# Batch 0's keys and values laid nine tokens to a partition, loaded on one queue, with v cast on the engines and the key sums taken as a column of v

## The chip, the core and the metric

The kernel runs on one core of a Trainium2 chip. The metric is device time in microseconds, the median of the runs. Five engines work side by side, each through its own list of instructions: TensorE (PE, with its weight loads as PEld), VectorE (DVE), ScalarE (ACT), GpSimd (POOL) and SyncE (SP). Sixteen DMA engines move data for all of them; a transfer is issued by an engine and then runs on its own.

## The reference

Inputs are q, k and v of shape (8 batches, 8 heads, 576 tokens, 64), a scale vector g of 512 and two weight matrices (512 x 2048 and 2048 x 512), all float32.

```python
q_s = exp(q) / sum over the 64 columns of a head
k_s = exp(k) / sum over the 576 tokens        # for each head and column
kv  = k_s^T v                                 # 64 x 64 for each batch and head
x   = q_s kv, heads side by side              # 8 x 576 x 512
xn  = (x - mean) / sqrt(var + 1e-6) * g       # over the 512 columns
out = x + relu(xn @ w1) @ w2
```

The maxima that the reference takes off before exp cancel in the quotients, and the kernel leaves them out.

## The kernel before

A batch is worked on as four tiles of 128 tokens (512 tokens, a partition holding four tokens in a row); the last 64 tokens of all eight batches form a ninth group, `C9`. For each batch the kernel builds kv, then x, then x normalised and transposed (`xnT`), and runs the two layers of the MLP. From batch 1 on the products of the layers are combined from seven instead of eight block products (lines 762 and 604); the first batch uses plain products (`mm1_part`, line 520, and `mm2_stream`, line 556). The order on every engine is the order in which the code issues (a manual schedule): `run(main, side)` walks the list of an MLP's matmuls, each with a weight, and issues side work when the sum of weights reaches the work's position.

What comes first is written out by hand in `first_batch`. Only there, batch 0's kv takes all 576 tokens at once: k and v lie six tokens to a partition (`T0 = 6`, so 96 partitions).

- SP issues q of tiles 0 and 1 (line 970) and then k, two heads a time (line 980). POOL waits for q by a small copy into `gate` (line 1004), and then issues v, cast to bfloat16 on the way (line 1006), q's tiles 2 and 3, and the weights: w1's first 512 columns in two halves of rows (line 1013), the rest of w1 and w2 (`load_w1`, `load_w2`), and the loads of batch 1.
- TensorE warms up on zeros (`warm`, line 867). ScalarE takes exp of q and of k. VectorE normalises q of tiles 0 and 1 (`norm_q`), and `eq_pT` transposes them on TensorE (line 928) into `eqT`.
- `z0_mm` (line 306) forms the key sums: exp(k) against a column of ones, six matmuls for each pair of heads; `recip_z` takes the reciprocals. `kv0_mm` (line 321) multiplies exp(k) and v of two heads into a 128x128 product, of which only the two diagonal 64x64 blocks are wanted; one VectorE instruction (line 322) scales it, masks it by `diag` and sums each row. That row sum becomes `mbc` (lines 327 and 331), a 128x128 matrix of -sum/512, by which a matmul takes off the mean of x.
- `xT_mm` (line 342) forms x minus its mean, already transposed, for tiles 0 and 1; `xT_out` (lines 351 and 353) writes it to `xnT` times g: column blocks 0 and 1 on VectorE, 2 and 3 on ScalarE.
- Tiles 2 and 3 of q come later: `eq_pT`, then `q0_rest(t)` (`z_q`, line 940, sums exp of q on TensorE from `eqT`, and `po_mm`, line 414, forms x), `x_fast` (line 464), `x_normed` and `xn_pT`.

The first layer of batch 0 (`mlp_steps(0)`) begins with 16 matmuls on tiles 0 and 1, of which the first eight use w1's first half of rows (kh=0) and the next eight the second half (kh=1); then block 0 for tile 2, then "the second block" (columns 512 to 1023 of w1, tiles 0 and 1), then block 0 for tile 3, and so on. A matmul of this layer has weight 0.5 for two tiles, so position 4 in the side list is after the first eight.

Of the kernel before, what the change touches and what calls it, by code (L numbers as in the profile page):

```python
# [20 lines left out]
def kernel(  # L21
# [50 lines left out]
    ident = const.tile([P, P], BF16)  # L72
    eps_ln = const.tile([P, 1], FP32)
    gate = const.tile([P, 4], FP32)
    ones = const.tile([P, 1], BF16)
    junk = const.tile([P, P], BF16)
    scrap = const.tile([P, 512], BF16)
    bones = const.tile([P, 2], BF16)
    ones_w = const.tile([P, P], BF16)
    diag = const.tile([P, P], FP32)  # L80
    mbc = const.tile([P, NP, P], BF16)
# [204 lines left out]

    kvbox = {}

    def exp_k0(j):
        hs = slice(2 * j, 2 * j + 2)  # L290
        if j == 0:
            eks[0] = raw.tile([P, T0, H, D], BF16, tag="kt", name="ek0", bufs=1)
        nc.scalar.activation(
            eks[0][0:P0, :, hs, :].rearrange("p t h d -> p h t d"), raws[0][0][0:P0, hs], AF.Exp
        )

    def k0_mm(j, t):
        hs = slice(2 * j, 2 * j + 2)
        return eks[0][0:P0, t, hs, :], raws["v0"][0:P0, hs, t, :], P

    def z0_mm(j):

        if j == 0:
            kvbox["z0"] = mm_ps.tile([P, NP], FP32, tag="m", name="z0")
        for t in range(T0):
            nc.tensor.matmul(
                kvbox["z0"][:, j : j + 1], k0_mm(j, t)[0], ones[0:P0],
                start=(j == 0 and t == 0), stop=(t == T0 - 1), skip_group_check=True,
            )

    def recip_z():
        kvbox["rz"] = sml.tile([P, NP], FP32, tag="rzk", name="rzk")
        kvbox["sum"] = sml.tile([P, NP], FP32, tag="lnv", name="kvs")
        nc.vector.reciprocal(kvbox["rz"], kvbox["z0"])

    def kv0_mm(j):
        pool, tag = (att_ps, "a") if j < 2 else (mm_ps, "m")
        pkv = pool.tile([P, P], FP32, tag=tag, name="pkv")
        for t in range(T0):
            lhsT, rhs, w = k0_mm(j, t)  # L320
            nc.tensor.matmul(pkv[:, 0:w], lhsT, rhs, start=(t == 0), stop=(t == T0 - 1))
        nc.vector.scalar_tensor_tensor(
            kv_sb[:, 0, j, :], in0=pkv, scalar=kvbox["rz"][:, j : j + 1], in1=diag,
            op0=ALU.mult, op1=ALU.mult, accum_out=kvbox["sum"][:, j : j + 1],
        )
        if j < NP - 1:
            nc.scalar.activation(
                mbc[:, j], ones_w, AF.Copy, scale=kvbox["sum"][:, j : j + 1]
            )
        else:  # L330
            nc.vector.tensor_scalar_mul(
                out=mbc[:, j], in0=ones_w, scalar1=kvbox["sum"][:, j : j + 1]
            )
# [21 lines left out]
    halves = (slice(0, 64), slice(64, P))  # L355

    def kv_pairs(b, ts=range(T + 1)):

# [501 lines left out]
        for _, fn in side[done:]:  # L860
            fn()

    def warm(n):

        w = mm_ps.tile([P, 4, P], FP32, tag="m", name="warm")
        for _ in range(n):
            nc.tensor.matmul(w, junk, junk[:, 0:4].to_broadcast([P, 4, P]), start=True, stop=True)

    def prep_fast(b):

# [74 lines left out]
    def eq_pT(c, t, eng):  # L945
        pe_T(eqTs[c], eqs[c][0][:, t].rearrange("p h d -> p (h d)"), t, eng)
# [10 lines left out]
    def first_batch():  # L957

        nc.scalar.preload_act_table_set("natural_log_exp_and_others")
        raws[0] = (  # L960
            mlp.tile([P, H, T0, D], FP32, tag="hT", name="kt0", bufs=1), None,
            raw.tile([P, H, T, D], FP32, tag="qt", name="qt"),
        )
        k0, _, q0 = raws[0]
        v0 = mlp.tile([P, H, T0, D], BF16, tag="hs", name="v0", bufs=1)
        raws["v0"] = v0

        def load_q0(t, tn, eng):
            ts = slice(t, t + tn)
            eng.dma_start(  # L970
                q0[:, :, ts],
                q[0, :, 0:SM, :].rearrange("h (p t) d -> p h t d", t=T)[:, :, ts],
            )

        def src0(x, h0, hn):
            return x[0, h0 : h0 + hn].rearrange("h (p t) d -> p h (t d)", t=T0)

        load_q0(0, 2, nc.sync)
        for h0 in range(0, H, 2):
            nc.sync.dma_start(  # L980
                k0[0:P0, h0 : h0 + 2].rearrange("p h t d -> p h (t d)"), src0(k, h0, 2)
            )
        raws["g"] = outp.tile([KO1, P], FP32, tag="ot", name="g_rows")
        nc.scalar.dma_start(
            raws["g"], bass.AP(moe_g_ln.tensor, moe_g_ln.offset, [[P, KO1], [1, P]])
        )
        nc.vector.memset(junk, 0.0)
        nc.vector.memset(eps_ln, 1e-6)
        nc.vector.memset(ones, 1.0)
        nc.vector.memset(bones, 0.0)  # L990
        nc.vector.memset(bones[0:64, 0:1], 1.0)
        nc.vector.memset(bones[64:P, 1:2], 1.0)
        nc.vector.memset(ones_w, -1.0 / DM)
        nc.vector.memset(diag, 0.0)
        for ps in halves:
            nc.vector.memset(diag[ps, ps], 1.0)
        nc.vector.memset(kv_sb[:, 1:B], 0.0)
# [7 lines left out]
        for h0, hn in ((0, 4), (4, 2), (6, 2)):  # L1005
            nc.gpsimd.dma_start(  # L1006
                v0[0:P0, h0 : h0 + hn].rearrange("p h t d -> p h (t d)"), src0(v, h0, hn)
            )
        for t in range(2, T):
            load_q0(t, 1, nc.gpsimd)  # L1010
# [17 lines left out]
        for j in range(NP):  # L1028
            exp_k0(j)
            z0_mm(j)  # L1030
            if j == NP - 2:
                g_columns()
        recip_z()
        kv0_mm(0)
        kv0_mm(1)
        kv0_mm(2)
        xT_mm(0, 0)
        kv0_mm(3)
        exp_qt(0, 2)
        exp_qt(0, 3)  # L1040
        xT_mm(1, 0)
        xT_mm(2, 0)
        xT_mm(0, 1)
        xT_mm(3, 0)
        xT_out(0)
        xT_out(1)
        eq_pT(0, 2, nc.scalar)
        xT_mm(1, 1)
        xT_mm(2, 1)
        eq_pT(0, 3, nc.vector)  # L1050
        xT_mm(3, 1)
        xT_out(2)
        xT_out(3)

    def q0_rest(t):
        z_q(0, t)
        for i in range(NP):
            po_mm(0, t, i)
# [33 lines left out]
    with tc.manual_schedule(  # L1092
# [11 lines left out]
        def po_x(c, t):  # L1104
            for i in range(NP):
# [85 lines left out]
```

## Time and profile before

| What | us |
|---|---|
| median of 3 runs (262.25 to 262.44) | 262.32 |
| the profiled execution | 262.09 |
| its span in the profile | 260.3 |
| TensorE busy | 253.9 |
| VectorE busy | 223.1 |
| ScalarE busy | 177.5 |
| GpSimd busy | 103.2 |

The profile is one execution. A row of the timeline gives the start, the time from there to the end of the merged instructions, the engine, the line of the code, the operation, what it writes and reads, the shape, and how often; in brackets stands the idle time ahead of it and what ended it. Ends of matmuls are modelled (0.27 us for a 256-column matmul whose neighbours start 0.109 apart), so spacing is read from starts. In the windows each engine has its busy time and number of instructions; the last three columns are TensorE's granted clock, the busy share of the DMA engines (it can exceed 1 where packets overlap) and GB/s. TensorE's clock rises to its full rate at 4.22 us and stays there.

### The profile page before, as it was taken

How to read it: one execution, taken by the hardware profiler on the slowest of the kernel's cores; microseconds unless marked ns; L12 is line 12 of the kernel's file. 1: busy time of each engine (PE TensorE's matmuls, PEld its weight loads, DVE VectorE, ACT ScalarE, POOL GpSimd, SP SyncE). 2: the span in 40 equal slices, each digit the busy share in tenths (PEclk: the TensorE clock that was granted, in tenths of full speed). 3: DMA queues.
4: the chain of work that ended last, by engine and by line, in shares of the span. 5: the costliest groups of instructions: out<-in, count | busy, mean ns of one | idle time of the engine just before them, and what ended most of it. 6: DMA issues, size and time to landing. Idle time of an engine off the chain costs nothing.

```text
span 260.3 us, 7286 instructions
## 1 busy us (share of the span) xinstructions
PE 253.9 (98%) x2885; PEld 215.6 (83%) x2885; DVE 223.1 (86%) x542; ACT 177.5 (68%) x348; POOL 103.2 (40%) x160
## 2 busy tenths in 40 slices
PE   8899999999999999999999999999999999999993
PEld 3689755788888888888888988888889888888883
DVE  6768996989989998899889988998899889957873
ACT  4747790997988685888588858885788386647400
POOL 3953247410299409800980098008200900190000
PEclk9999999999999999999999999999999999999999
DMA  6999999988699995999699859989902630422014
GB/s 198 257 203 208 354 221 332 257 169 308 118 122 321 268 120 107 300 247 107 142 300 235 86 135 304 232 89 161 279 0 50 142 137 1 77 71 99 3 40 121
DMA packets 82618, 45.04 MB, mean 173 GB/s; under 512 B 58196, under 2 KB 79192, under 8 KB 82584
## 3 DMA queue, kind: packets, MB, share of 16 engines
q0 software_dynamic: 32464, 21.76, 45.8%
q1 hardware_dynamic: 49488, 22.29, 36.8%
q10 hardware_dynamic: 632, 0.53, 0.7%
q8 instruction: 22, 0.36, 0.6%
q14 instruction: 12, 0.10, 0.1%
HBM read 36.70 MB, written 9.44 MB: 177 GB/s over the span
## 4 chain that ended last, share of the span: by engine, by line
PE 92%; DMA 4%; POOL 2%; DVE 0%; issue 0%
PE ba L604 21%; PE bx L762 20%; PE bb L762 10%; PE ph L520 8%; PE bb L604 6%; PE be L604 5%; PE bc L604 5%; PE pc L556 5%; PE bc L762 5%; DMA w_raw<-in_moe_w_ch_dram 3%; PE pkv L371 2%; DMA qt<-in_q_dram 2%; PE po L403 2%; PE ptr L928 1%; PE po L414 1%; POOL v L1006 1%
## 5 line engine op out<-in xcount | busy, mean ns | idle before, releaser
L604 PEld LDWEIGHTS <-hs 128*128 128x128 bf16 x512 | 49.6, 98 | 6.0
L269 POOL TENSOR_TENSOR tq<-xnT 128x256 bf16<-128x256 bf16 x30 | 20.1, 671 | 85.3 <-PE bc L604 73.9
L762 PEld LDWEIGHTS <-w_raw 128*128 128x128 bf16 x480 | 46.7, 98 | 5.5
L604 PEld LDWEIGHTS <-hT 128*128 128x128 bf16 x392 | 37.6, 98 | 4.2
L762 PEld LDWEIGHTS <-w1g 128*128 128x128 bf16 x360 | 34.7, 98 | 4.3 <-issue 0.2
L762 PE MATMUL bx<-tq,w_raw 128*128 128x256 bf16 x240 | 31.3, 273 | 0.0
L604 PE MATMUL ba<-w_q,hs 128*128 128x256 bf16 x256 | 30.6, 273 | 0.0
L786 ACT COPY bc<-bx 128x512 f32<-128x512 f32 x30 | 16.7, 596 | 19.1 <-PE bx L762 19.1
L427 ACT ACTIVATE scrap<-x,mv 128x512 bf16<-128x512 bf16 x32 | 23.1, 723 | 4.6 <-DVE mv L457 4.4
L793 DVE TENSOR_TENSOR bb<-bx,s 128x512 f32<-128x512 f32 x30 | 19.5, 694 | 7.2 <-ACT s L790 4.5
L804 ACT ACTIVATE hT<-bb 128x512 bf16<-128x512 f32 x30 | 16.3, 595 | 9.3 <-PE bb L762 9.3
L804 ACT ACTIVATE hT<-bc 128x512 bf16<-128x512 f32 x30 | 16.5, 595 | 8.5 <-PE bc L762 8.5
L796 DVE TENSOR_TENSOR hT<-bx,s 128x512 bf16<-128x512 f32 x30 | 19.3, 684 | 3.2 <-PE bx L762 3.1
L587 DVE TENSOR_TENSOR hs<-hT 128x1024 bf16<-128x1024 bf16 x32 | 21.4, 672 | 0.5 <-ACT hT L804 0.5
L229 DVE TENSOR_REDUCE zq<-eq 128x16 f32<-128x1024 bf16 (+1 forms) x20 | 20.7, 1049 | 0.5 <-ACT eq L220 0.5
L269 POOL TENSOR_TENSOR tq<-xnT,tq 128x256 bf16<-128x256 bf16 x30 | 20.0, 669 | 1.1
L449 DVE SCALAR_TENSOR_TENSOR x<-po,rq 128x256 bf16<-128x256 f32 x48 | 17.5, 420 | 1.7 <-PE po L403 1.7
L790 ACT COPY s<-bb 128x512 f32<-128x512 f32 x30 | 16.6, 622 | 0.0
L804 ACT ACTIVATE hT<-bx 128x512 bf16<-128x512 f32 x30 | 16.4, 610 | 0.0
L762 PE MATMUL bx<-xnT,w1g 128*128 128x256 bf16 x120 | 16.2, 273 | 0.0
L762 PE MATMUL bx<-tq,w1g 128*128 128x256 bf16 x120 | 15.9, 272 | 0.0
L762 PE MATMUL bc<-xnT,w1g 128*128 128x256 bf16 x120 | 15.8, 273 | 0.0
(157 smaller groups left out, 535.0 us busy)
## 6 DMA issues: line engine op xcount, KB each, us to landing
out_dram<-ot POOLq DMA_DIRECT2D x30, 256.0 KB, 4.4
kt<-in_k_dram SPq DMA_DIRECT2D x5, 1024.0 KB, 11.6
qt<-in_q_dram SPq DMA_DIRECT2D x4, 1024.0 KB, 9.9
qt<-in_q_dram POOLq DMA_DIRECT2D x2, 1024.0 KB, 12.7
kt<-in_k_dram POOLq DMA_DIRECT2D x2, 1024.0 KB, 14.5
vm<-in_v_dram POOLq DMA_DIRECT2D x16, 128.0 KB, 12.4
qt<-in_q_dram SPq DMA_DIRECT2D x3, 512.0 KB, 5.7
w_raw<-in_moe_w_ch_dram POOLq DMA_DIRECT2D x3, 512.0 KB, 10.5
```

Of the source, the lines that this page charges most:

```text
L229: nc.vector.reduce_sum(eqs[c][1][:, ts], eqs[c][0][:, ts], axis=AX.X)
L269: nc.gpsimd.tensor_tensor(out=dst[:, t], in0=x[:, t], in1=y[:, t], op=ALU.subtract)
L427: nc.scalar.activation(scrap, x[:, t], AF.Square, bias=mv[:, t, 0:1], scale=-float(DM), accum_out=mv[:, t, 1:2],)
L449: nc.vector.scalar_tensor_tensor(x[:, t].rearrange("p (i two d) -> p i two d", two=2, d=D)[:, :, half], in0=pobox[c, t][half], scalar=1.0, ...
L520: nc.tensor.matmul(ph[:, m % 2, at : at + tn], (w1g if c else w1_sb)[:, ko, m * P : (m + 1) * P], xnTs[c][:, t0 : t0 + tn, ko, :], start=( ...
L587: nc.vector.tensor_tensor(out=dst, in0=x, in1=y, op=op)
L604: nc.tensor.matmul(hbox[bank][:, t, cs], lhsT, rhs[:, cs], start=first and (own or t == 0) and k == 0, stop=k == KH - 1, skip_group_check= ...
L762: nc.tensor.matmul(dst[:, q], lhsT, rhs, start=first and q == 0 and ko == 0, stop=ko == 1, skip_group_check=True)
L786: nc.scalar.copy(at[g, "c"], at[g, "x"])
L793: nc.vector.tensor_tensor(out=at[g, "b"], in0=at[g, "x"], in1=at[g, "s"], op=ALU.add)
L796: nc.vector.tensor_tensor(out=h_out(g, 1, 1), in0=at[g, "x"], in1=at[g, "s"], op=ALU.add)
L804: nc.scalar.activation(h_out(g, odd, half), at[g, name], AF.Relu)
```

## The change

Batch 0's k and v are laid nine tokens to a partition: two heads fill 128 partitions, 64 for each head (`T0 = 9`). k and v are both loaded by SP in float32, a pair of heads at a time, and the rest of q behind them on the same queue; the `gate` copy is gone. v is cast to bfloat16 into a buffer with a 65th column of ones: pairs 0 and 1 on POOL, ahead of its weight issues, pair 2 on ScalarE, pair 3 split over VectorE and ScalarE. The product of a head is 64x65 over 64 partitions; its last column is the key sum, and the two heads of a pair go to two PSUM banks. `kv0_out` takes the reciprocals and writes the two 64x64 blocks, one on ScalarE and one on VectorE, each summing its rows; the mean is taken off with a single column `kvm`, broadcast as weights. `xT_out` alternates between the engines. Seven of the first warm-up matmuls are float32. The transposes of tile 3's q move into the first layer (position 3), `q0_rest(3)` goes from position 4 to 5.

The core of the diff:

```diff
-    T0 = 6
-    P0 = S // T0
+    T0 = 9
...
     def exp_k0(j):
...
+        nc.scalar.activation(eks[0][:, j], raws[0][0][:, j], AF.Exp)
+
+    def cast_v0(j, eng, ts=slice(0, T0)):
+        dst, src = raws["v0"][:, j, ts, 0:D], raws["v32"][:, j, ts]
...
+    def kv0_mm(j):
+
+        pool, tag = ((att_ps, "a"), (mm_ps, "m"))[j % 2]
+        banks = [pool.tile([P, VW], FP32, tag=tag, name="pkv") for _ in halves]
+        for t in range(T0):
+            for ps, bank in zip(halves, banks):
+                nc.tensor.matmul(
+                    bank[ps], eks[0][ps, j, t], raws["v0"][ps, j, t],
+                    start=(t == 0), stop=(t == T0 - 1), skip_group_check=True,
+                )
...
+    def kv0_out(j):
...
+        nc.vector.reciprocal(rz[qs], hi[qs, D:])
+        nc.vector.reciprocal(rz[ps], lo[ps, D:])
         nc.scalar.activation(
+            kv_sb[qs, 0, j, qs], hi[qs, 0:D], AF.Copy, scale=rz[qs], accum_out=total[qs]
+        )
         nc.vector.scalar_tensor_tensor(
+            kv_sb[ps, 0, j, ps], in0=lo[ps, 0:D], scalar=rz[ps], in1=ones_f[ps],
+            op0=ALU.mult, op1=ALU.mult, accum_out=total[ps],
+        )
+        nc.vector.tensor_scalar_mul(out=kvm[:, j : j + 1], in0=total, scalar1=-1.0 / DM)
...
-        ops += [(mbc[:, j], i) for i in range(2)]
+        ops += [(kvm[:, j : j + 1].to_broadcast([P, P]), i) for i in range(2)]
...
-        if i < 2:
+        if i % 2 == 0:
...
-        load_q0(0, 2, nc.sync)
+        load_q0(0, 2)
+        for dst, x in ((k0, k), (v32, v)):
+            for j in range(NP):
+                load_pair(dst, x, j)
         for h0 in range(0, H, 2):
+            load_q0(2, 2, slice(h0, h0 + 2))
...
-        nc.gpsimd.tensor_copy(out=gate, in_=q0[:, 1, 0, 0:4])
...
+        for j in range(2):
+            cast_v0(j, nc.gpsimd)
         for kh in range(2):
             ks = slice(2 * kh, 2 * kh + 2)
             nc.gpsimd.dma_start(w1_sb[:, ks, 0:512], w1_src[:, ks, 0:512])
...
-        warm(17)
+        warm(7, junk_f)
+        warm(2)
         for t in range(2):
             exp_qt(0, t)
             norm_q(0, t)
         eq_pT(0, 0, nc.vector)
+        for j in range(NP):
+            exp_k0(j)
         warm(6)
         eq_pT(0, 1, nc.vector)
+        g_columns()
         kv0_mm(0)
+        kv0_out(0)
+        cast_v0(2, nc.scalar)
         kv0_mm(1)
+        xT_mm(0, 0)
+        xT_mm(0, 1)
+        kv0_out(1)
+        cut = slice(0, 4), slice(4, T0)
+        cast_v0(3, nc.vector, cut[0])
+        cast_v0(3, nc.scalar, cut[1])
         kv0_mm(2)
+        kv0_out(2)
+        xT_mm(1, 0)
+        xT_mm(1, 1)
         kv0_mm(3)
+        kv0_out(3)
+        xT_mm(2, 0)
+        xT_mm(2, 1)
+        xT_mm(3, 0)
+        xT_mm(3, 1)
         exp_qt(0, 2)
+        for i in range(NP):
+            xT_out(i)
+            if i == 1:
+                exp_qt(0, 3)
+        eq_pT(0, 2, nc.vector)
+        warm(2)
...
                 (2, lambda: (q0_rest(2), x_fast(0, 2), x_normed(2))),
-                (4, lambda: q0_rest(3)),
+                (3, lambda: eq_pT(0, 3, nc.scalar)),
+                (5, lambda: q0_rest(3)),
                 (6, lambda: (xn_pT(0, 2, nc.vector), x_fast(0, 3), x_normed(3))),
```

More of the change, by code (lines that the diff above doesn't have):

```diff
@@ L74 @@
     gate = const.tile([P, 4], FP32)
-    ones = const.tile([P, 1], BF16)
     junk = const.tile([P, P], BF16)
+    junk_f = const.tile([P, P], FP32)
     scrap = const.tile([P, 512], BF16)
     bones = const.tile([P, 2], BF16)
-    ones_w = const.tile([P, P], BF16)
-    diag = const.tile([P, P], FP32)
-    mbc = const.tile([P, NP, P], BF16)
+    ones_f = const.tile([P, D], FP32)
+    kvm = const.tile([P, NP], BF16)
     g_one = const.tile([P, KO1], FP32)
@@ L287 @@
     kvbox = {}
+    halves = (slice(0, 64), slice(64, P))
     def exp_k0(j):
-        hs = slice(2 * j, 2 * j + 2)
         if j == 0:
-            eks[0] = raw.tile([P, T0, H, D], BF16, tag="kt", name="ek0", bufs=1)
+            eks[0] = raw.tile([P, NP, T0, D], BF16, tag="kt", name="ek0", bufs=1)
+        nc.scalar.activation(eks[0][:, j], raws[0][0][:, j], AF.Exp)
+    def cast_v0(j, eng, ts=slice(0, T0)):
+        dst, src = raws["v0"][:, j, ts, 0:D], raws["v32"][:, j, ts]
+        if eng is nc.scalar:
+            nc.scalar.copy(dst, src)
+        else:
+            eng.tensor_copy(out=dst, in_=src)
@@ new lines, in kv0_mm @@
+    def kv0_mm(j):
[7 more added lines that the diff above has]
+                )
+        kvbox["kv0", j] = banks
+    def kv0_out(j):
+        if j == 0:
+            kvbox["rz"] = sml.tile([P, NP], FP32, tag="rzk", name="rzk")
+            kvbox["sum"] = sml.tile([P, NP], FP32, tag="lnv", name="kvs")
+        (lo, hi), rz, total = kvbox["kv0", j], kvbox["rz"][:, j : j + 1], kvbox["sum"][:, j : j + 1]
+        ps, qs = halves
+        nc.vector.reciprocal(rz[qs], hi[qs, D:])
+        nc.vector.reciprocal(rz[ps], lo[ps, D:])
@@ L293, in exp_k0 @@
         nc.scalar.activation(
-            eks[0][0:P0, :, hs, :].rearrange("p t h d -> p h t d"), raws[0][0][0:P0, hs], AF.Exp
+            kv_sb[qs, 0, j, qs], hi[qs, 0:D], AF.Copy, scale=rz[qs], accum_out=total[qs]
         )
[L297 to L321, printed above, removed]
@@ L322, in kv0_mm @@
         nc.vector.scalar_tensor_tensor(
-            kv_sb[:, 0, j, :], in0=pkv, scalar=kvbox["rz"][:, j : j + 1], in1=diag,
-            op0=ALU.mult, op1=ALU.mult, accum_out=kvbox["sum"][:, j : j + 1],
-        )
[L326 to L333, printed above, removed]
+            kv_sb[ps, 0, j, ps], in0=lo[ps, 0:D], scalar=rz[ps], in1=ones_f[ps],
@@ L353, in xT_out @@
             nc.scalar.activation(dst, src, AF.Copy, scale=g_one[:, i : i + 1])
-    halves = (slice(0, 64), slice(64, P))
     def kv_pairs(b, ts=range(T + 1)):
@@ L861, in run, with warm @@
             fn()
-    def warm(n):
+    def warm(n, src=junk):
         w = mm_ps.tile([P, 4, P], FP32, tag="m", name="warm")
         for _ in range(n):
-            nc.tensor.matmul(w, junk, junk[:, 0:4].to_broadcast([P, 4, P]), start=True, stop=True)
+            nc.tensor.matmul(w, src, src[:, 0:4].to_broadcast([P, 4, P]), start=True, stop=True)
     def prep_fast(b):
@@ L960, in first_batch @@
         raws[0] = (
-            mlp.tile([P, H, T0, D], FP32, tag="hT", name="kt0", bufs=1), None,
+            mlp.tile([P, NP, T0, D], FP32, tag="hT", name="kt0", bufs=1), None,
             raw.tile([P, H, T, D], FP32, tag="qt", name="qt"),
@@ L964, in first_batch, with load_q0, load_pair @@
         k0, _, q0 = raws[0]
-        v0 = mlp.tile([P, H, T0, D], BF16, tag="hs", name="v0", bufs=1)
-        raws["v0"] = v0
-        def load_q0(t, tn, eng):
+        v32 = mlp.tile([P, NP, T0, D], FP32, tag="hs", name="v32", bufs=1)
+        raws["v32"], raws["v0"] = v32, raw.tile([P, NP, T0, VW], BF16, tag="qt", name="v0")
+        def load_q0(t, tn, hs=slice(0, H)):
             ts = slice(t, t + tn)
-            eng.dma_start(
-                q0[:, :, ts],
-                q[0, :, 0:SM, :].rearrange("h (p t) d -> p h t d", t=T)[:, :, ts],
-            )
-        def src0(x, h0, hn):
-            return x[0, h0 : h0 + hn].rearrange("h (p t) d -> p h (t d)", t=T0)
-        load_q0(0, 2, nc.sync)
+            nc.sync.dma_start(
+                q0[:, hs, ts],
+                q[0, hs, 0:SM, :].rearrange("h (p t) d -> p h t d", t=T)[:, :, ts],
+            )
+        def load_pair(dst, x, j):
+            nc.sync.dma_start(
+                dst[:, j].rearrange("p t d -> p (t d)"),
+                x[0, 2 * j : 2 * j + 2].rearrange("two (s t) d -> (two s) (t d)", t=T0),
+            )
[3 more added lines that the diff above has]
+                load_pair(dst, x, j)
         for h0 in range(0, H, 2):
-            nc.sync.dma_start(
-                k0[0:P0, h0 : h0 + 2].rearrange("p h t d -> p h (t d)"), src0(k, h0, 2)
-            )
+            load_q0(2, 2, slice(h0, h0 + 2))
         raws["g"] = outp.tile([KO1, P], FP32, tag="ot", name="g_rows")
@@ L992, in first_batch @@
         nc.vector.memset(bones[64:P, 1:2], 1.0)
[L993 to L997, printed above, removed]
+        nc.vector.memset(ones_f, 1.0)
+        nc.vector.memset(raws["v0"][:, :, :, D:], 1.0)
+        nc.vector.memset(kv_sb, 0.0)
         nc.vector.memset(vr, 0.0)
```

29 lines of the change are left out of this document (1 added, 28 removed).

## The prediction

> **What bounds the kernel now.** I read the page first (busy shares, chain), then the chain of the first 20 us, TensorE's timeline there, the waits, and the DMA rates in windows. The page:
>
> ```profile
> PE 253.9 (98%) x2885; PEld 215.6 (83%) x2885; DVE 223.1 (86%) x542; ACT 177.5 (68%) x348; POOL 103.2 (40%) x160
> PE 92%; DMA 4%; POOL 2%; DVE 0%; issue 0%
> ```
>
> TensorE is busy 98% of the span and 92% of the chain; only about 16 us at the start hang on something else. Starts of its matmuls show gaps of over 0.06 us beyond streaming only seven times between 16.8 and 60 us, 0.7 us in all. So the change, which touches batch 0 alone, pays what it does to the time at which TensorE enters that dense stretch. The chain of the first 20 us:
>
> ```profile
> 0.74 4.29 DMA qt<-in_q_dram
> ...
> 5.27 2.07 POOL v L1006 x3
> 7.33 1.84 POOL qt L970 x2
> ...
> 9.82 6.86 DMA w_raw<-in_moe_w_ch_dram
> 16.68 0.05 issue
> 16.72 0.61 PE ph L520 x4
> ```
>
> The gate is the landing of w1's second half (kh=1) at 16.68. And TensorE just ahead of it:
>
> ```profile
> 14.62 0.60 PE L520 MATMUL ph<-xnT,w_raw 128*128 128x256 bf16 x4
> ...
> 15.93 0.38 PE L414 MATMUL po<-kv_sb,eqT 128*128 128x128 bf16 x4
> 16.72 0.61 PE L520 MATMUL ph<-xnT,w_raw 128*128 128x256 bf16 x4 [0.41 <-DMA w_raw<-in_moe_w_ch_dram]
> ```
>
> Counted from starts, its issue idled from 16.15 to 16.72, 0.57 us (the 0.41 in the brackets counts from the modelled end of po); the attention chain for the first two q tiles was done that much before w1. The first layer's second block starts at 19.57 (its 16 matmuls and everything after them run dense); I use that start as the yardstick: what shifts it shifts the end.
>
> **The transfers.** They fill the DMA engines from 2 to 45 us, so order and rate count:
>
> ```profile
> 4.00:5.00 1.00, 1.00 (x6) 0.44 (x5) 0.93 (x1) 0.00 (x0) 0.00 (x0) 1.00 1.12 376
> 6.00:7.00 1.00, 0.43 (x2) 0.00 (x0) 0.93 (x3) 0.93 (x2) 1.00 (x3) 1.00 1.06 281
> 30.00:32.00 2.00, 2.00 (x16) 1.34 (x14) 2.00 (x4) 0.61 (x2) 0.57 (x1) 1.00 1.03 408
> ```
>
> The last column is GB/s. At 6 to 7 us only k's 96-partition loads run: 281, so a pair of heads (0.295 MB) takes 1.02 to 1.05 us (its exps start 1.03 apart). On 128 partitions q of batch 0 (4 to 5 us, same queue) shows 376 and batch 1's q 408: 0.78 or 0.72 us. I take 0.78; bounds 0.72 and 1.05. The Trainium skill's page "SBUF — State Buffer" (section on door 1, the DMA port swizzle) gives 436 GB/s over all 16 ports; by that a pair would take 0.68 us, an estimate. v now costs 2.6 us (landings 9.12 to 11.72, cast on the way); as float32 it costs four more pairs. q's rest goes from 1.47 us to 0.52 MB at the 342 GB/s that q's first load shows at 3 to 4 us: 1.53.
>
> Landings: q 5.03 as before; k ends at 5.03 + 4 x 0.78 = 8.15 (9.12 now); v pairs at 8.93, 9.71, 10.49, 11.27; q's rest by 12.80 (13.19 now). The issues waiting for free lanes on SP (v's third for q, q's rest for k) are all served by landings that come earlier, so nothing idles behind them. But on POOL all of w1's and w2's issues and batch 1's loads now stand behind two casts, and so TensorE's gate does. POOL's copy of 1024 elements takes 1167 ns and one of 4 takes 186, so 576 cost 0.74 us: v0 cast at 9.70, v1 at 10.45. w1's first issue then starts at 10.45 instead of 9.13. The first software transfer moved data 2.5 us after its issue began (5.21 to 7.72), so w1's data would begin at 12.95, against 13.19 now: 0.24 us earlier, kh=1 at 16.44. One 16 KB packet of the instruction queue (15.90, 0.95 us) delayed the last of its sixteen parts from 15.71 to 16.68; I count it as staying, bounds -0.95 and 0.
>
> **The chain from v to x.** Removed: 24 key-sum matmuls (0.025 each, 0.6), three mbc copies on ScalarE, one on VectorE, and 24 wide products (0.055 each, 1.3). Added: 72 matmuls of 64x65. The later kv_pairs (128-row, 64x65) start two per 0.03 us, so 18 take 0.28; upper bound one per 0.055, 1.0. TensorE is ready at 9.5 (transposes to 9.2, gcp 0.3); v0 is cast at 9.70; products stand at 9.75 + 0.28 + 0.2 drain = 10.23. The warm-up rewritten as 7 float32 matmuls + 2 must end by 7.42; see the rivals.
>
> Then VectorE and ScalarE alternate, four times: reciprocal 0.18, ScalarE's 64-wide evacuation (0.40 for 128x128 with a scale, 0.21 for reading the accumulator, overlapping by 0.13; less for half the width: 0.44), hand-overs 0.08, then kvm before the next reciprocal: 0.77 a pair, and 0.85 for the last through kvm. Into that queue go the casts: v2 on ScalarE (512 elements take 0.60) costs 0.25 beyond its slack, v3 in two parts 0.25. kvm of the last pair: 10.23 + 3 x 0.77 + 0.85 + 0.5 = 13.89. Now the last mbc stands at 13.02. Bounds: 0.60 a pair and casts hidden (13.0), 0.95 a pair and single matmuls (15.3).
>
> Five pxT matmuls follow (0.109 each): pxT ready at 14.3 and 14.6 (14.79 for the second now). The evacuations are alternated: x_out 0 on VectorE to 14.8, x_out 1 on ScalarE behind the exp of q tile 2, which waits for the rest of q (12.80, before the engine is there); transposes of q tile 2 and two warms (2 x 0.217) fill TensorE to 15.1, where the first layer starts, 0.47 later than now. Up to kh=1: 8 matmuls 0.87, q0_rest(2) 0.33, moved transposes of tile 3 0.22, 0.1 for a copy that is late behind x_out 2: 16.6. Now 16.72. So w1 (16.44) no longer ends last; the chain does.
>
> Behind the gate the reordering costs: q0_rest(3) was at position 4, in front of the kh=1 matmuls and inside the idle time; at 5 it is behind two of them: 4 x 0.025 + 4 x 0.055 = 0.33 us of TensorE in the open. It needs eqT of tile 3, whose copy on ScalarE (0.57) starts after transposes at about 16.4: ready 17.2, TensorE there at 16.85: 0.35 idle. Against that stands the arrival 0.12 earlier. Second block: 19.57 - 0.12 + 0.33 + 0.35 = 20.13, +0.56 us.
>
> The rest is free: memsets end before 5.7 as now (kv_sb 1.55 grows by 0.2, diag's four go); the copy of kvm as a broadcast weight reads one column (uncovered it costs at most 0.05 a load, 0.8 over 16); POOL's later issues have lanes at the same distance; w1's next block lands 2.6 after kh=1, at 19.0, under 20.0.
>
> The sum is against the profiled execution: 262.09 (span 260.3, and 1.8 around it that the change leaves alone) + 0.56 = 262.65; the median of the runs, 262.32, stands 0.23 above the profiled one, so 262.9.
>
> **Rivals.** (1) The float32 warm-up is longer. The only float32 product here:
>
> ```profile
> 0.99 5.43 PE L867 MATMUL warm<-junk 128*128 128x512 bf16 x17 [0.99 <-DVE bones L990]
> ...
> 9.73 0.38 PE L953 MATMUL gcp<-ident_f,g_rows 4*128 4x4 f32 x2
> ```
>
> One instruction leaves two load/matmul pairs. At one pass a pair, 7 float32 equal 14 of the 17 warms: end 6.1. If each pair streams twice, 28 passes: 7.5 at 0.427 until the clock rises at 4.22, 20.5 at 0.217, end 8.7, with two bf16 9.1. Then transposes, six warms (1.3) and transposes put TensorE at v0 not at 9.75 but at 11.15: up to 1.4 later, 0.2 regained, 264.1. For: nothing in the trace excludes it, as four moving columns are too few to time a pass. Against: two pairs are recorded, not four. The Trainium skill's page "FP8 and Floating Point Precision" (TensorE Precision Notes) says true FP32 takes 4 passes through the array; by that rule this rival holds. No run here shows it yet.
>
> (2) Loads on 128 partitions are no faster (1.02 a pair): v1 at 11.15, casts, issue at 11.9, w1's data at 14.4, 1.2 later, and q0_rest(3) in the open: 263.9. Against: 376 and 408 GB/s.
>
> (3) Faster: the loop runs at 0.6 a pair, and the instruction packet misses kh=1 (landing 15.5). TensorE passes the gate at 15.6, pays 0.33 behind it: 16.72 - 15.6 - 0.33 = 0.8 us gained, 261.5. It decides where the first layer's first matmul starts before 14.3. For: v lands earlier, no key-sum pass. Against: v needs a cast and the loop has four hand-overs.
>
> (4) Both cancel, within 0.2%: the loop at 0.65 a pair brings the first layer to 14.6, and 262.3 stays.
>
> **Numbers.** Forecast (+0.2 to +1.1) 0.38, rival 1 0.22, rival 2 0.08, rival 3 0.25, rival 4 alone 0.07. 0.2% of the time, 0.5 us, is about what a measurement of this kernel can tell from no change. Half of the forecast lies inside it with rival 4: same 0.25. Slower: the other half and rivals 1 and 2: 0.48. Faster 0.27. The range takes rivals 1 to 3 at their prices, rival 3 with loads of 0.72 us a pair (five to v0, 0.3 less): 261.2 to 264.2; the forecast's own is 262.5 to 263.4.
>
> **What would show it.** Right: first w1 matmuls near 15.1, no wait on w1 at kh=1, a short wait of zs on eqT's copy, second block at 20.0 to 20.2. k exps about 0.8 apart. Wrong: warm ending at 9 (rival 1), first layer before 14.3 (rival 3), or TensorE again waiting for w1.

## The result, and the profile after

Six runs of the changed kernel have a median of 266.10 us (265.26 to 267.51), six of the kernel before 262.40 (262.25 to 262.55): a ratio of 1.0144, 95% interval 1.0116 to 1.0172. It is slower by 3.7 us (1.4%), above the range of the prediction (261.2 to 264.2). The profiled run took 265.65, with a span of 263.9 against 260.3.

Two lines of the page of the changed kernel, busy times and the chain by engine:

```profile
PE 257.3 (98%) x2907; PEld 216.7 (82%) x2910; DVE 223.8 (85%) x551; ACT 178.3 (68%) x355; POOL 100.6 (38%) x156
PE 97%; DVE 1%; issue 0%; ACT 0%; DVEq 0%
```

TensorE stands for 97% of the chain instead of 92%, and the 4% of DMA are gone from it: the start of the kernel, which hung on transfers, now hangs on TensorE itself. The chain of the first 24 us of the changed kernel (start, length, what):

```profile
1.05 8.91 PE warm L861 x16
9.96 0.22 PE ptr L922 x4
10.19 1.30 PE warm L861 x6
...
12.02 0.42 PE pkv L307 x18
12.47 0.17 DVE rzk L320
12.67 0.17 DVE rzk L321
12.87 0.29 DVE kv_sb L325 x2
...
19.37 0.59 ACT eqT L924
20.01 0.25 PE zs L934 x4
```

Before, this chain ran through the loads and ended in w1 at 16.68. Now its first 9 us are the warm-up on zeros, and no transfer stands in it. TensorE's timeline says the same:

```profile
1.05 8.47 PE L861 MATMUL warm<-junk_f 128*128 128x512 f32 x14 [1.05 <-DVE junk_f L985]
9.37 0.59 PE L861 MATMUL warm<-junk 128*128 128x512 bf16 x2
9.80 0.38 PE L922 MATMUL ptr<-ident,eq 128*128 128x128 bf16 x4
...
11.95 0.77 PE L307 MATMUL pkv<-v,ek 64*64 64x65 bf16 x36
...
17.82 0.75 PE L514 MATMUL ph<-xnT,w_raw 128*128 128x256 bf16 x4
...
22.97 1.25 PE L514 MATMUL ph<-xnT,w_raw 128*128 128x256 bf16 x10
```

The seven float32 matmuls leave 14 records. Counted from starts, each instruction takes 1.71 us at first and 0.86 later, where a bf16 matmul of the same 512 columns takes 0.427 and 0.217: four passes each. The warm-up, which ended one microsecond before it was needed (6.42 against 7.42), now ends at 9.80 and holds up all that follows; exp(q) and v's first two pairs are ready by then (v landed at 8.34 and 9.10, and the casts end at 9.82, 2.1 before the products begin at 11.95). The second block, the yardstick, starts at 22.97 instead of 19.57. From there to the end the trace adds 0.2 (a lag of 3.4 grows to 3.6 at 46 us), and 3.6 is the difference of the spans.

### The profile page after: what moved, and what is told of

The parts are those of the page before. It is cut to its first block, busy times and chain, and to the rows that moved or that the text cites. A ratio compares the mean times of both kernels' runs of the same rounds, so it can differ in the third digit from the quotient of the medians.

```text
span 263.9 us, 7365 instructions
## 1 busy us (share of the span) xinstructions
PE 257.3 (98%) x2907; PEld 216.7 (82%) x2910; DVE 223.8 (85%) x551; ACT 178.3 (68%) x355; POOL 100.6 (38%) x156
## 4 chain that ended last, share of the span: by engine, by line
PE 97%; DVE 1%; issue 0%; ACT 0%; DVEq 0%
PE ba L598 21%; PE bx L756 20%; PE bb L756 10%; PE ph L514 8%; PE bb L598 6%; PE be L598 5%; PE bc L598 5%; PE pc L550 5%; PE bc L756 5%; PE warm L861 4%; PE pkv L365 2%; PE po L397 2%; PE ptr L922 1%; PE po L408 1%; PE pxT L338 1%; PE pkv L307 0%
```

## The experiments

Theory A: the float32 warm-up streams in four passes and makes TensorE late. The rivals: B, later called V, the chain of small steps behind v on VectorE; and L, the order and start of the transfers. Each ratio is against runs of the kernel before made beside it (medians 262.03 to 262.53). "Products" is the start of batch 0's k-v products, "last sum" that of the last scaled key sum (for the kernel before, of the last `mbc`), all in us, from the profiled run.

| kernel | products | last sum | first layer | second block | median | ratio to before, interval |
|---|---|---|---|---|---|---|
| before | 10.22 | 12.77 | 14.62 | 19.57 | 262.40 | |
| after | 11.95 | 16.39 | 17.82 | 22.97 | 266.10 | 1.0144 (1.0116 to 1.0172) |
| e1_bf16_warm | 9.25 | 13.90 | 15.33 | 20.47 | 263.78 | 1.0045 (1.0023 to 1.0066) |
| e2_before_f32_warm | 12.51 | 15.05 | 16.91 | 21.51 | 264.15 | 1.0059 (1.0039 to 1.0080) |
| e3_bf16_warm_early_q | 9.24 | 13.68 | 14.98 | 20.10 | 263.72 | 1.0035 (1.0010 to 1.0061) |
| e4_f32_equal_width | 9.75 | 14.34 | 15.77 | 20.95 | 263.73 | 1.0052 (1.0032 to 1.0072) |
| e5_w1_early | 9.43 | 13.87 | 15.30 | 20.44 | 263.38 | 1.0042 (1.0025 to 1.0059) |
| e6_w1_early_q | 9.38 | 13.83 | 15.01 | 20.05 | 262.98 | 1.0026 (1.0009 to 1.0042) |
| e7_casts_pool | 9.23 | 13.66 | 14.85 | 20.20 | 263.22 | 1.0043 (1.0020 to 1.0065) |
| e8_one_bank | 9.61 | 14.92 | 16.14 | 21.14 | 263.85 | 1.0061 (1.0037 to 1.0086) |
| e9_banks_order | 9.86 | 14.10 | 15.29 | 20.39 | 263.25 | 1.0033 (1.0009 to 1.0058) |
| e10_kvm_act | 9.38 | 13.70 | 15.02 | 19.73 | 262.65 | 1.0022 (1.0001 to 1.0043) |
| e11_sums_ahead | 10.17 | 14.12 | 16.66 | 21.48 | 264.13 | 1.0076 (1.0048 to 1.0103) |
| e12_pairs_in_turn | 7.07 | 12.90 | 14.88 | 21.02 | 264.47 | 1.0086 (1.0067 to 1.0105) |

### The warm-up taken out, put in, and made as wide as before

e1, from the changed kernel:

```diff
-        warm(7, junk_f)
-        warm(2)
+        warm(17)
```

> The changed kernel with the warm-up of before (seventeen bf16 matmuls in place of seven float32 and two bf16). Theory A, the float32 warm-up streams each matmul in four passes and so ends at 9.80 us instead of 6.42, and TensorE reaches batch 0's v late: the warm-up ends at about 6.4 again, the first product of k and v stands as soon as the first cast lets it, near 9.3 instead of 11.95, everything behind it moves by the same 2.65, the last of the four key sums comes near 13.8 instead of 16.39, the first-layer matmuls begin near 15.2 instead of 17.82, the second block near 20.2 to 20.4 instead of 22.97, and the time is 262.9 to 263.3. Theory B, the chain of small VectorE steps behind v (about 1.0 us a pair) and the order of the loads cost the time whatever the warm-up does: the first product moves, but the second block stays near 23 and the time near 266.

e2, from the kernel before:

```diff
+    junk_f = const.tile([P, 64], FP32)
...
-        warm(17)
+        warm(7, junk_f)
+        warm(2)
```

> The kernel before with the warm-up of after (seven float32 and two bf16 matmuls) and nothing else; the float32 warm-up writes 64 rows instead of 128 for want of SBUF, with the same 512 columns streamed. Theory A (four passes): the warm-up ends near 9.8, the first transposes of exp(q) come at 9.8 instead of 7.42, 2.4 us later; the wait for w1's second half (0.64 us, from 16.09 to 16.73) swallows a part, so the second block starts 1.8 later, near 21.3, and the time is about 264.1. Theory B (the warm-up is not what costs): the second block stays near 19.6 and the time at 262.4.

e4, from the changed kernel:

```diff
-        warm(7, junk_f)
-        warm(2)
+        warm(4, junk_f)
+        warm(1)
```

> The changed kernel with four float32 and one bf16 warm-up matmuls instead of seven and two. Theory A, four passes to a float32 matmul: 4 x 4 + 1 = 17 passes, the same stream as the seventeen bf16 matmuls, so the warm-up ends at 6.4 to 6.5 and the time is that of the kernel with the bf16 warm-up within 0.3. If a float32 matmul streams in two passes (two records each), this is 9 passes: it ends near 4.8, before the clock has risen, and TensorE waits for exp(q). Theory B: no change from 266.

All three came out as theory A has it, with two misses in size: e1's time is 0.5 above the range it was given, and e4's warm-up ends at 7.6 and not at 6.5. With e1 the excess over the kernel before falls from 3.7 to 1.3 us, and the products start 2.70 earlier. e2, which gives the kernel before this warm-up and nothing else, costs 1.7 us. TensorE's timeline of e2:

```profile
0.99 8.39 PE L868 MATMUL warm<-junk_f 128*64 128x512 f32 x14 [0.99 <-DVE junk_f L988]
...
9.76 0.38 PE L929 MATMUL ptr<-ident,eq 128*128 128x128 bf16 x4
...
18.43 0.60 PE L521 MATMUL ph<-xnT,w_raw 128*128 128x256 bf16 x4
```

The transposes come at 9.76 instead of 7.42, 2.34 late. The kernel before has an idle stretch ahead of w1's second half, and that takes 0.6 of it: the row at 18.43 has no wait in brackets, and stands 1.71 later than the 16.72 of before. e4's four float32 matmuls and one bf16 are 17 widths at four passes, and time and products come within 0.05 us and 0.5 us of e1's, with seventeen bf16. Two passes would have made nine widths. The warm-up of e4 with the transposes that follow it, and then that of e1, whose transposes start at 7.10:

```profile
1.05 6.49 PE L861 MATMUL warm<-junk_f 128*128 128x512 f32 x8 [1.05 <-DVE junk_f L985]
...
7.60 0.38 PE L922 MATMUL ptr<-ident,eq 128*128 128x128 bf16 x4
```

```profile
1.13 6.13 PE L861 MATMUL warm<-junk 128*128 128x512 bf16 x17 [1.13 <-DVE bones L988]
```

So the float32 warm-up accounts for 2.4 of the 3.7 us (266.10 less 262.40, against 263.78 less 262.44).

### Where the other 1.3 us are: q and w1

A part of the 1.3 us lies outside the profile's span. In the kernel before, the device time exceeds the span by 1.8 us (by at most 1.86 in the 35 runs beside e1), in single runs of e1 by up to 3.06; the medians of the spans, 261.75 and 260.7, differ by 1.05. What takes the rest no run shows.

e3, from e1: the exps of q's tiles 2 and 3 and their transposes back among the pairs.

```diff
         kv0_out(2)
+        exp_qt(0, 2)
...
         kv0_out(3)
+        exp_qt(0, 3)
...
+        eq_pT(0, 2, nc.vector)
         xT_mm(3, 0)
...
-        warm(2)
+        eq_pT(0, 3, nc.scalar)
...
-                (3, lambda: eq_pT(0, 3, nc.scalar)),
-                (5, lambda: q0_rest(3)),
+                (4, lambda: q0_rest(3)),
```

> The changed kernel with the bf16 warm-up, and with the rest of q put back among the pairs: exp of q's blocks 2 and 3 behind the outputs of pairs 2 and 3, their transposes ahead of the first-layer matmuls, the two filling matmuls there left out, the last sums of q back at position 4. Theory A: the first-layer matmuls begin near 14.8, the 0.5 us gap for the last copy of exp(q) transposed is gone, and w1's second half (landing at 16.34 in the changed kernel) is about what gates them; the second block starts near 19.2, 0.3 to 0.4 ahead of before, and the time is about 262.0. Theory B (the chain behind v sets the time): as the kernel with the bf16 warm-up alone, or 266 if that stays there.

The first layer starts 0.35 earlier and nothing there waits for `eqT`, but the second block starts only 0.37 earlier, because w1's second half lands at 17.21, not at 16.34, and the time does not move. Later a wait of batch 1 appears:

```profile
17.25 0.61 PE L514 MATMUL ph<-xnT,w_raw 128*128 128x256 bf16 x4 [0.31 <-DMA w_raw<-in_moe_w_ch_dram]
...
34.26 0.40 PE L922 MATMUL ptr<-ident,eq 128*128 128x128 bf16 x4 [0.24 <-ACT eq L218]
```

The prediction for e3 was wrong by 1.7. e5, from e1, and e6, from e3, start w1 earlier:

```diff
-        for j in range(2):
-            cast_v0(j, nc.gpsimd)
+        nc.gpsimd.tensor_copy(out=gate, in_=v32[:, 0, 0, 0:4])
         for kh in range(2):
...
             exp_k0(j)
+        for j in range(2):
+            cast_v0(j, nc.scalar)
```

> The changed kernel with the bf16 warm-up, the casts of v's pairs 0 and 1 moved from POOL to ACT (idle from 8.2 to 9.9 there), and POOL's issues of w1 gated by a small copy on the landing of v's pair 0 instead of standing behind two casts: first issue near 8.4 instead of 9.6. Theory L (of the 1.3 us that stay above the kernel before, a part is w1's late start, which leaves the transfers thin from 12 to 16 us, and the later landings of batch 1): w1's halves land near 13.3 and 15 to 16 instead of 14.5 and 17.2, the first layer's second half is no longer waited for (0.57 less), the second block starts near 19.9 instead of 20.47, and the time is 263.0 to 263.2 against 263.8. Theory V (only the VectorE chain behind v costs): second block within 0.2 of 20.47, 263.8.

> The same move of w1's issues and the two casts, in the kernel with the bf16 warm-up and the rest of q put back among the pairs. Theory L: no wait for w1's second half (0.5 less than the 17.25 seen), the second block near 19.7 instead of 20.10, and the wait of the transposes of batch 1's exp(q) at 34.3 (0.24) gone because its loads land earlier: 262.5 to 262.9. Theory V: within 0.2 of the kernel without the move, 263.7.

w1's halves land at 13.36 and 15.25 in e5 (14.48 and 17.21 in e1), as theory L has it, and the wait for them is gone; but then the last sums of q wait for `eqT` (0.24), and the second block stays (20.44 against 20.47). In e6, where neither stands in the way, it is 20.05, and the wait at 34 us is gone: 262.98, just above what was expected. e5's 263.38 lies between the two theories. The intervals of e3 and e6 overlap, as do those of e1 and e5. So w1's place behind two casts costs something in the transfers, and by itself nothing that stands clear of the intervals.

### The chain behind v

e7, from e6: pairs 2 and 3 cast on POOL, behind w1's first two issues.

```diff
+        for j in range(2, NP):
+            cast_v0(j, nc.gpsimd)
         for nb in range(1, 4):
...
-        cast_v0(2, nc.scalar)
...
-        cast_v0(3, nc.vector, cut[0])
-        cast_v0(3, nc.scalar, cut[1])
```

> The kernel before this in the list, with the casts of v's pairs 2 and 3 on POOL (0.72 each, behind w1's two issues, done by about 11.5) instead of ACT and VectorE. Theory V (VectorE's chain sets the pitch of the pairs, 0.28 of it this cast, and the casts on ACT delay pair 1's outputs): the last key sum comes about 0.3 earlier, near 13.5, the second block 0.2 to 0.3 earlier. Theory L alone: no change, and POOL's later issues, 1.4 behind, would land later.

e8, from e7: one bank, one reciprocal, the scaled sum on ScalarE.

```diff
-        banks = [pool.tile([P, VW], FP32, tag=tag, name="pkv") for _ in halves]
+        banks = [pool.tile([P, VW], FP32, tag=tag, name="pkv")] * 2
...
-        nc.vector.reciprocal(rz[qs], hi[qs, D:])
-        nc.vector.reciprocal(rz[ps], lo[ps, D:])
+        nc.vector.reciprocal(rz, lo[:, D:])
...
-        nc.vector.tensor_scalar_mul(out=kvm[:, j : j + 1], in0=total, scalar1=-1.0 / DM)
+        nc.scalar.activation(kvm[:, j : j + 1], total, AF.Copy, scale=-1.0 / DM)
```

> As the kernel before this in the list, with both 64x64 products of a pair in one bank, one reciprocal of 128 rows in place of two of 64, and the scaled key sum made on ACT instead of VectorE. Theory V: VectorE's part of a pair falls from about 1.0 to 0.6 us, TensorE's own 0.95 a pair then sets the pitch, the last key sum comes 0.3 to 0.5 earlier still, near 13.1, and the time is 0.2 to 0.5 less than that of the kernel before this in the list, near 262.0 to 262.3. Theory L alone: no change. If two products in one bank get in each other's way on TensorE, the 18 matmuls of a pair take more than the 0.48 of now.

e7's last sum comes 0.17 earlier, but TensorE then waits 0.42 for a row of x and the second block is 0.15 later than in e6: no gain. e8 went the wrong way. VectorE in e8:

```profile
10.13 0.17 DVE L320 RECIPROCAL rzk<-pkv 128x1 f32<-128x1 f32 x1 [0.41 <-PE pkv L307]
10.76 0.28 DVE L324 SCALAR_TENSOR_TENSOR kv_sb<-pkv,rzk,ones_f 64x64 bf16<-64x64 f32 x1 [0.47 <-ACT kv_sb L321]
```

With both products in one bank, VectorE's half waits until ScalarE has read the other half (idle for 0.47 to 0.97 in each pair, longest where the exp of q's tile 2 stands ahead on ScalarE). In two banks they read side by side: in the changed kernel ScalarE starts at 12.68 and VectorE at 12.87. Whether the chip needs that wait, or only the program has it, no run shows. The 18 matmuls of a pair take 0.48 in either form.

e9, from e7: x's blocks shared out so that the two read at once lie in different banks, and products ahead of sums. e10, from e9: the scaled sum on ScalarE as in e8.

```diff
-        ops = [(kv_sb[:, 0, j, :], j % 2)] if j // 2 == kh else []
+        ops = [(kv_sb[:, 0, j, :], j // 2)] if j % 2 == kh else []
...
-        dst, src = xnTs[0][:, 0:2, i, :], pobox["T", i // 2][:, i % 2]
+        dst, src = xnTs[0][:, 0:2, i, :], pobox["T", i % 2][:, i // 2]
...
+        kv0_out(1)
+        kv0_mm(2)
         xT_mm(0, 0)
```

> The kernel with all four casts off VectorE, with two edits behind it: the four blocks of x transposed shared out over the two banks so that the block VectorE reads and the block ACT reads at the same time lie in different banks (in the changed kernel they share one, and ACT's read starts 0.52 after VectorE's, when that is done), and the products of pairs 2 and 3 issued ahead of the sums of pairs 0 and 1. Theory V: VectorE no longer waits for the products of pair 2 (0.12 and 0.12 there), ACT's read starts with VectorE's, the first-layer matmuls run without the 0.24 gap, and the second block starts 0.4 to 0.6 earlier than the 20.20 without the edits, near 19.7: 262.4 to 262.8. Theory L (transfers set it): no change, 263.2.

> The kernel before this in the list with the scaled key sum on ACT instead of VectorE, in two banks this time. Theory V: VectorE's part of a pair falls from 0.98 to about 0.78, the last key sum comes 0.3 to 0.5 earlier unless the exp of q's blocks 2 and 3 on ACT stands in its way (0.63 each), the second block near 19.3: about 262.0 to 262.3. If ACT becomes the bound, as in the kernel with one bank, the last key sum is later and the time 263 or more.

e9 missed. Its profiled run began the products 0.63 later than e7's (the warm-up ran longer, see the last section); counted from there its last sum is 0.19 earlier and the first layer free of the 0.24 gap, but the medians are alike. e10 reached 262.65, short of the 262.0 to 262.3 expected, 0.2% above before with an interval that begins at 1.0001. VectorE in e10:

```profile
9.90 0.17 DVE L320 RECIPROCAL rzk<-pkv 64x1 f32<-64x1 f32 x1 [0.31 <-PE pkv L307]
...
10.62 0.17 DVE L320 RECIPROCAL rzk<-pkv 64x1 f32<-64x1 f32 x1
```

A pair takes 0.72 of VectorE here, against 0.98 in the changed kernel, and then VectorE waits for TensorE's products (0.37 and 0.38), of which the third pair's wait for POOL's cast of v (0.58). The last sum is held by ScalarE: its half of the last pair starts at 13.27, behind the exp of q's tile 2 (0.63 from 12.61), as the expectation allowed for.

### The other half undone, and the loads in turn

e11, from e9: v loaded as bf16 through POOL's queue, the key sums ahead of v from k alone.

```diff
+        nc.gpsimd.tensor_copy(out=gate, in_=q0[:, 1, 0, 0:4])
+        for j in range(NP):
+            load_pair(v0, v, j, nc.gpsimd)
+        for t in range(2, T):
+            load_q0(t, 1, nc.gpsimd)
...
+            z0_mm(j)
+        warm(2)
         eq_pT(0, 1, nc.vector)
         g_columns()
+        for j in range(2, NP):
+            z0_mm(j)
+        recip_z()
```

> The kernel with shared-out banks and products issued ahead, keeping the nine tokens to a partition and the 64x64 products in two banks, but with the other half of the change undone: v is loaded as bf16 through POOL's queue (four pair loads behind a copy on q's landing, q's blocks 2 and 3 and w1 behind them as before), no engine casts, and the key sums are made ahead of v from k alone with a column of ones (72 more small matmuls in place of four of the six filling ones), one reciprocal for all pairs. Theory V (the casts and the reciprocals behind v are what the new form pays): VectorE's part of a pair falls from 0.98 to about 0.6, TensorE's 0.95 a pair then sets the pitch, the last key sum comes near 12.6 instead of 14.1, the first-layer matmuls begin near 14.0 to 14.3, held by w1's first half, the second block near 19.0, and the time is 261.5 to 262.0, ahead of before by 0.2 to 0.7. Theory L (transfers set it): bf16 v through POOL lands no earlier than before by more than the 1.5 that k gains, w1's second half lands near 15.5 to 16.5, second block 19.2 to 19.6, and the time is that of before within 0.3.

e12, from the changed kernel, with e1's warm-up and e9's banks (the rest of q stays late, as in the changed kernel): loads in turn, casts and scaled sums on POOL.

```diff
-        for dst, x in ((k0, k), (v32, v)):
-            for j in range(NP):
+        for j in range(NP):
+            for dst, x in ((k0, k), (v32, v)):
...
-        nc.vector.tensor_scalar_mul(out=kvm[:, j : j + 1], in0=total, scalar1=-1.0 / DM)
+        nc.gpsimd.tensor_scalar_mul(
+            out=kvm[:, j : j + 1], in0=kvbox["sum"][:, j : j + 1], scalar1=-1.0 / DM
+        )
```

> The changed kernel with the bf16 warm-up and the loads of k and v in turn (k pair 0, v pair 0, k pair 1, ...) instead of four k and then four v: same bytes, so v's pairs land near 6.1, 7.6, 9.1 and 10.35 instead of 8.3, 9.1, 9.8 and 10.35. All casts on POOL, the scaled key sums on POOL, w1's first half issued between the casts, the columns of g made during the warm-up, x's transposed blocks shared out over two banks. Theory V (TensorE reaches the first layer late because the chain behind v runs four times in a row after the last load): three of the four turns now lie beside the loads, the last key sum comes near 12.9 instead of 14.1, the first-layer matmuls begin near 14.0, the second block near 18.8, and the time is 261.4 to 261.9, ahead of before. Theory L (the transfers of w1 set it): the first layer waits for w1's first half near 13.7 and its second half near 15.5, second block 19.2 to 19.6, 262.0 to 262.5. If VectorE, which makes exp(q)'s norms until 8.4, is the bound: the last key sum near 13.4 to 13.8, no gain over the kernel without it, 262.5 to 263.

Both were to beat the kernel before, and in both TensorE waits for a transfer. TensorE in e11, and then in e12:

```profile
16.66 0.61 PE L518 MATMUL ph<-xnT,w_raw 128*128 128x256 bf16 x4 [1.38 <-DMA w_raw<-in_moe_w_ch_dram]
```

```profile
21.02 1.16 PE L518 MATMUL ph<-xnT,w_raw 128*128 128x256 bf16 x9 [0.79 <-DMA w_raw<-in_moe_w_ch_dram]
```

In e11 the pairs of bf16 v land at 9.54, 10.34, 11.12 and 11.92, as late as in the kernel before (10.18 to 11.72) although k is done 1.3 earlier, and w1's first half lands at 16.61. So the engine casts are not waste: v in float32, queued behind k, lands 1.2 to 1.6 us earlier (8.34 to 10.35), and its first two pairs are cast by 9.11 and 9.82, still 0.4 to 0.5 ahead of e11's. With the reciprocals ahead of v, e11's first three scaled sums follow each other at 0.45 and 0.56 instead of 0.97; the fourth comes at 14.12, because ScalarE's half stands behind the exp of q's tile 2, which waits for q until 13.01. The profiled run of e11 (266.14) is 2.0 above its median; half of its loss against the kernel before comes after the second block, so only the start is read here. In e12 the products begin at 7.07 and the last sum 0.76 earlier than in e7, but w1's next columns, issued by POOL at 13.3 behind all casts and sums (11.3 in the changed kernel), land at 21.0. The transfers are not all that the two lose: without these waits, and nothing else moved, the second block would stand near 19.9 in e11 (21.48 less 1.55 between starts) and near 20.1 in e12 (its last transposes start at 19.84 and take 0.22), estimates from the rows, against 19.57 before. Neither was tried without its wait. No kernel here beats the kernel before.

## Why the prediction was wrong

The yardstick was forecast at 20.13 and stood at 22.97. By the steps of the sum:

| step | forecast | measured | difference |
|---|---|---|---|
| TensorE at v, products begin | 9.75 | 11.95 | +2.20 |
| from there to the end of the last key sum | 4.14 | 4.60 | +0.46 |
| to the first layer | 1.21 | 1.27 | +0.06 |
| first layer to kh=1 | 1.5 | 1.57 | +0.07 |
| kh=1 to the second block | 3.53 | 3.58 | +0.05 |

In the changed kernel kh=1 begins at 19.39, the ninth matmul of the layer.

**The step that failed** is the one that let the warm-up end by 7.42, "at one pass a pair". Rival 1 had the mechanism, at 0.22, and e1, e2 and e4 show it. The Trainium skill's page "FP8 and Floating Point Precision" (TensorE Precision Notes) has true FP32 as four passes; the trace agrees, 0.86 us against 0.217 for 512 columns. The argument against it, that two pairs are recorded and not four, was no evidence: each of the two records streams twice. Four columns of `gcp` could not show that, and the prediction said so, but then gave the reading with the lower price the larger chance.

**Rival 1 was too cheap**, 264.1 against 266.1. It let the pitch of the warm-up (the time from one matmul's start to the next) halve at 4.22 as in the kernel before; in this run it halves at 5.49, and the warm-up ended at 9.80, not 9.1. And it added nothing of the loop's upper bound: a late TensorE and a loop of more than 0.77 a pair add up, so that the range had to reach both at once.

**The loop** is the second term. It was sized at 0.77 a pair, and runs at 0.97, 1.18 and 0.97. VectorE in the changed kernel, one pair:

```profile
12.47 0.17 DVE L320 RECIPROCAL rzk<-pkv 64x1 f32<-64x1 f32 x1 [0.16 <-PE pkv L307]
12.67 0.16 DVE L321 RECIPROCAL rzk<-pkv 64x1 f32<-64x1 f32 x1
12.87 0.28 DVE L325 SCALAR_TENSOR_TENSOR kv_sb<-pkv,rzk,ones_f 64x64 bf16<-64x64 f32 x1
13.08 0.08 DVE L325 DVE_READ_ACCUMULATOR kv_sb<-pkv,rzk,ones_f 64x1 f32 x1
13.27 0.16 DVE L329 TENSOR_SCALAR kvm<-kvs 128x1 bf16<-128x1 f32 x1
13.45 0.17 DVE L320 RECIPROCAL rzk<-pkv 64x1 f32<-64x1 f32 x1
```

VectorE, not the hand-over to ScalarE, sets the pace: its steps, 1 to 64 columns wide, start 0.18 to 0.21 apart. The forecast took one reciprocal a pair where the code has two. Part of the excess was hidden, since the casts of v cost the loop 0.21 (1.18 against 0.97) and not the 0.5 of the forecast. The old form needs one step and its accumulator read a pair on VectorE, as e2 shows with its products ready:

```profile
13.38 0.35 DVE L323 SCALAR_TENSOR_TENSOR kv_sb<-pkv,rzk,diag 128x128 bf16<-128x128 f32 x1
...
13.71 0.35 DVE L323 SCALAR_TENSOR_TENSOR kv_sb<-pkv,rzk,diag 128x128 bf16<-128x128 f32 x1
```

0.33 a pair against 0.98. Four times the difference is 2.6 us, part of which the earlier v pays for: with the bf16 warm-up the products begin 0.97 before those of the kernel before, and the last sum 1.13 after its last `mbc`. That this, with w1 and q behind it, makes up the 1.3 us of e1 is argued from the traces; no single edit shows it. Reordering q or w1 alone moved the time within the intervals; e6 and e10, which change several of these at once, come to 0.26% and 0.22%.

**What was right.** The loads: from q's landing at 4.61 to the third pair of v at 9.82 seven pairs take 0.74 each (forecast 0.78, bounds 0.72 and 1.05), at this rate (windows of the changed kernel, GB/s last):

```profile
6.00:7.00 1.00, 1.00 (x4) 0.49 (x3) 0.96 (x3) 1.00 (x3) 0.00 (x0) 1.00 1.04 403
...
12.00:13.00 1.00, 0.72 (x37) 0.61 (x36) 0.77 (x6) 0.32 (x2) 1.00 (x3) 1.00 1.26 118
```

Rival 2 is thereby out. A cast on POOL takes 0.72 (forecast 0.74), and w1 no longer ends last. That w1's second half lands at 16.34 (forecast 16.44) is luck: its first data move at 11.39 and not at 12.95, and the instruction packet, counted as staying, comes at 18.46, behind it; but the two halves take 4.95 from there where the forecast had 3.49, packet included. From 12 to 15 us nothing but w1 moves, at 118 to 158 GB/s, where the kernel before has 198 for w1 at 13 to 15; why it is slower there is not shown. The wait of the moved `q0_rest(3)` for ScalarE's copy of `eqT` came where it was forecast, 0.51 between starts, 0.40 of it idle, where 0.35 was forecast:

```profile
20.01 0.25 PE L934 MATMUL zs<-bones,eqT 128*128 128x2 bf16 x4 [0.24 <-ACT eqT L924]
```

Rival 3's condition, a loop of 0.6 a pair and the first layer before 14.3, was met by none of these kernels; e11's loop alone came under 0.6 for its first three pairs.

**Overlooked.** `xT_out` alternating between the engines puts two reads of one bank side by side, and they run in turn: ScalarE's starts at 17.56, 0.52 after VectorE's 17.04. With the blocks shared out over two banks (e9) it starts 0.32 after.

## What to carry to other kernels

A filler is work: price a change of its type by its passes, and ask what the slack behind it was, since it becomes the path as soon as that is used up (here 1.0 us of slack against 3.4 us of growth). Where a mechanism is not excluded by any row, the cheaper reading of a record count is no reason to make it the unlikely one, and the bounds of independent terms add in the range. Work moved behind the last load is paid at the pitch of its busiest engine, once a pair: count every small dependent instruction there (0.2 us each on VectorE) before counting what it saves elsewhere.

## What the runs showed of the hardware

The point at which TensorE's pitch halves is not fixed; the 4.22 us of the kernel before belong to that one execution. The same seventeen matmuls from 1.13 us on, in e3 and in e9:

```profile
1.13 5.40 PE L861 MATMUL warm<-junk 128*128 128x512 bf16 x17 [1.13 <-DVE bones L988]
```

```profile
1.13 6.74 PE L861 MATMUL warm<-junk 128*128 128x512 bf16 x17 [1.13 <-DVE bones L988]
```

From starts, the pitch goes from 0.427 to 0.217 at 4.3 us in e3 and at 7.0 in e9, and in e4 from 0.853 to 0.431 a record at 6.7, while the granted clock in the windows stands at 1.00 in all three. The Trainium skill's page "TensorE: Matmul & The Clock Gate" (What's actually happening) tells of a cold half rate and a free-running window; the two pitches agree with the first, and a spread of 2.8 us (4.28 in e3, 7.04 in e9) between kernels with the same start fits the second, though it is wider than the half microsecond either way that the page gives. The windows show no step in the granted clock, so the halving is read from the starts alone. Whether this is what spreads the times, the runs do not show: the six runs of the kernel before lie within 0.30 us and the six of the changed kernel within 2.25, but 35 other runs of the kernel before reach from 261.81 to 265.16, and the twelve of e2, whose warm-up is late too, lie within 1.38.

The landing of w1's second half also depends on where a 16 KB packet of the instruction queue, 0.95 us long, falls. It starts at 15.90 in the kernel before, 15.46 in e1 and 18.46 in the changed kernel; the half lands at 16.68, 17.21 and 16.34. In the kernel before, fifteen of the half's sixteen parts have landed by 15.71, and in e4, with the packet at 16.07, by 16.73; the last comes 0.97 and 1.00 later. What sets the packet's start is not shown. From the changed kernel to e1, where only the warm-up differs, it comes 3.0 earlier, with TensorE 2.5 to 2.7 earlier; but from e6 to e7 it moves from 16.05 to 14.08, while TensorE's first layer starts only 0.16 earlier. The sum of the prediction held this packet fixed, and its rival 3 let it miss.
